# One list for attention and MLP, eight PSUM banks in one stock, key copies by transfer: windowed attention, expert attention and MLP on one core

## The chip, the core and the metric

The kernel runs on one core of a Trainium2 chip. Four engines compute, each with its own instruction queue that is worked off in order: TensorE (PE: matrix multiplications and transposes; it writes only to PSUM, which has eight banks of 128 x 512 floats), VectorE (DVE), ScalarE (ACT) and GpSimd (POOL). SyncE (SP) issues the transfers (DMA). Engines wait for each other by semaphores. The metric is the device time of one execution in microseconds (us).

## What is computed

Three stages over 4 batches of 576 tokens; every result is float32.

```python
# 1: attention, 8 heads of 64: a window of 32, in heads 4 to 7 one of 128 with every fourth key
attn = softmax(mask(q @ k.T / 8)) @ v
x = attn.transpose(0, 2, 1, 3).reshape(B, S, 512)
# 2: four experts, the two with the larger logit of x @ w_gate weighted by a softmax
for e in range(4):
    a = softmax(causal((x @ wq[e]) @ (x @ wk[e]).T / 8))
    out += weight[e] * (a @ (x @ wv[e]) @ wo[e])
# 3: norm, MLP, residual; w_ch1 (512 x 2048) and w_ch2 (2048 x 512) are float64
xn = (out - mean) / sqrt(var + 1e-6) * g_ln
y = out + relu(xn @ w_ch1) @ w_ch2
```

## The kernel before

**Number format.** A product that needs full precision is three matmuls: both factors are kept as a high and a low part (xh and xl, KH and klz, ht's two halves), and high x high, high x low and low x high are summed in one PSUM bank. Each such result so costs a copy (the high part, ACT) and a subtraction (the low part, DVE).

**Stages.** For each batch: `loads` (L301) brings q, k and v by pairs of heads; `turned_qk` (L361) transposes q and k on PE; `window` (L410) does the local attention in three units for each pair: scores (L436), maximum and subtraction (L446, L448), exponential, division, transpose (L464), the product with v (L477), and the split into xh and xl (L495, L497). `value_tile` (L505) computes V and the gate's logits in five tiles, `gate` (L551) chooses the experts, `project` (L596) makes queries and keys of a pair of experts, `attend` (L668) does one query tile of expert attention, and `out_proj` (L820) the output projection. The MLP has 18 token tiles in five groups (four of 512 tokens, one of 256) and 16 slices f of the hidden width. `decode` (L884) loads a slice of float64 weights and turns its bits into two float32 parts by a chain of steps on ACT, DVE and POOL; `norm_tile` (L992) normalizes and transposes a token tile through one buffer xg; `mlp_group` (L1025) does a pair of slices for a group: phid (L1043), ht (L1051, L1053), pout (L1068), and the sum into x2 (L1075).

**The order of the work.** Most of the kernel is a set of Python generators. Each `yield op(engine, ns, deps)` is one step with a price, `acq` takes a buffer from a pool, `key` waits for a fact, `give` and `put` return buffers and state facts. `run_chains` (L198) is a list scheduler that runs when the program is built: among all steps that could go next it emits the one with the earliest start by its own clock; ties go to the lower rank of the chain. Nothing of it runs on the chip; there each engine follows the emitted order and real waits decide. An `acq` is granted by rank as soon as the pool has a place, even where the step behind it can only start later.

**PSUM pools.** The banks are three pools: a (3) for turned q and k, window transposes and outputs, the scores of batches 1 to 3, norm tiles and the early MLP; s (2) for the window scores of batch 0 and the expert scores; t (3) for values, projections, the attend transposes and outputs, and the output projection. The value tiles of batch 0 ask for a bank right after the key V, before x and the weights exist; those of later batches wait for x first.

**Key copies.** The keys of expert ee lie in one half of the partitions of the projection's bank and must stand in both halves of KH, since the queries' high and low parts are stacked on the partitions. ACT writes one half (L643), ACT or DVE the other (L644 and L645).

**The MLP.** Units in the list: f = 0 and 1 for groups 0 to 2, then f = 2 for groups 0 to 2. All other units and the decode of f = 3 to 15 are emitted after the list by a plain loop outside the hand-written order (from L1134 on), with two s banks for phid and three t banks for pout.

Of the kernel before, what the change touches and what calls it, by code (L numbers as in the profile page):

```python
# [23 lines left out]
def windowed_attention_moe_mlp(  # L24
# [15 lines left out]
    nc = tc.nc  # L40
# [115 lines left out]
    places = {"a": [0.0] * BANKS["a"], "s": [0.0] * BANKS["s"], "t": [0.0] * BANKS["t"]}  # L156
# [17 lines left out]
    def give(tag, at, n=1):  # L174
        places[tag] += [at] * n

# [21 lines left out]
    def run_chains():  # L198
        while chains:
            again = True  # L200
            while again:
                again = False
                for c in sorted(chains, key=lambda c: c[0]):
                    kind = c[2][0]
                    if kind == "acq" and len(places[c[2][1]]) >= c[2][2]:
                        tag, n = c[2][1:]
                        places[tag].sort()
                        at = places[tag][n - 1]
                        del places[tag][:n]
                        resume(c, at)  # L210
                        again = True
                        break
# [43 lines left out]
    def attention_weights(x):  # L256
# [20 lines left out]
        t += 4000.0  # L277
# [23 lines left out]
    def loads(b):  # L301
# [4 lines left out]
        for hp in range(NHP):  # L306
# [7 lines left out]
            for x, src in enumerate((q, k)):  # L314
# [20 lines left out]
            if not dil:  # L335
                for h in range(2):
                    vs = v[b, h0 + h]
                    yield op("SP", 500.0, [t])
                    nc.sync.dma_start(vt[W:96, 0, h], vs[0:64])
                    ti = yield op("SP", 900.0, [t])  # L340
# [12 lines left out]
            land[0] = max(ti + 700.0, land[0]) + 1000.0  # L353
# [7 lines left out]
    def turned_qk(b, hp):  # L361
# [12 lines left out]
        for x in range(4):  # L374
            nat, hf = nats[x // 2], x % 2
            ta = yield acq("a")
            pt = bank("a", "ptr")
# [22 lines left out]
            give("a", t)  # L400
# [9 lines left out]
    def window(b, hp, u):  # L410
# [8 lines left out]
        tag = "s" if b == 0 else "a"  # L419
        ta = yield acq(tag)  # L420
        ps = bank(tag, "s1")
# [27 lines left out]
        give(tag, t)  # L449
# [10 lines left out]
        ta = yield acq("a")  # L460
        pt = bank("a", "ppt")
# [8 lines left out]
        give("a", t)  # L470
        ta = yield acq("a")
        po = bank("a", "po")
# [20 lines left out]
        for c0, m, sl in pieces:  # L493
            th = yield op("ACT", act(m), [t, tx])
            nc.scalar.copy(xh[:, hp, sl], po[:, c0:c0 + m])  # L495
            tl = yield op("DVE", dve(m), [th])
            nc.vector.tensor_tensor(xl[:, hp, sl], po[:, c0:c0 + m], xh[:, hp, sl].bitcast(F32), op=ALU.subtract)  # L497
        give("a", tl)
# [6 lines left out]
    def value_tile(b, i):  # L505
# [5 lines left out]
        tb = yield acq("t")  # L511
        pv = bank("t", "pv")
# [29 lines left out]
        give("t", t)  # L542
# [8 lines left out]
    def gate(b):  # L551
# [25 lines left out]
        for s in steps:  # L577
            t = yield op("DVE", 100.0, [t])
            s()
# [16 lines left out]
    def project(b, pr_):  # L596
# [18 lines left out]
        for hf in range(2):  # L615
            for wh, wl, isq in ((wkh, wkl, False), (wqh, wql, True)):
                tb = yield acq("t")
                pp = bank("t", "pp")
# [11 lines left out]
                ends = []  # L630
                for ee in range(2):
# [9 lines left out]
                    else:  # L641
                        a = yield op("ACT", 392.0, [t, tq])
                        nc.scalar.copy(KH[ee][own, cs], pp[own, :HS])  # L643
                        a2, e = yield either(("ACT", 392.0), ("DVE", 380.0), deps=[t, tq])  # L644
                        copy_by(e, KH[ee][oth, cs], pp[own, :HS])  # L645
# [3 lines left out]
                        a = max(a, a2)  # L649
                    ends.append(a)  # L650
                give("t", max(ends))
                put("q", b, pr_, hf, isq, at=max(ends))
# [15 lines left out]
    def attend(b, pr_, i):  # L668
# [19 lines left out]
        for ee in range(2):  # L688
            cuts = [(0, n)] if n <= 512 else [(0, 64), (64, n)]
            tb = yield acq("s", len(cuts))  # L690
            pss, tss = [], []
            for a, z in cuts:
                ps = bank("s", "s2")
# [6 lines left out]
                pss.append(ps)  # L700
# [14 lines left out]
            else:  # L715
# [11 lines left out]
                give("s", t, len(cuts))  # L727
                t = yield op("DVE", 75.0, [t])
                nc.vector.tensor_reduce(sm[:m, ee:ee + 1], s2[:m], axis=AX.X, op=ALU.add)
            if len(cuts) == 1:  # L730
                give("s", t)
# [16 lines left out]
        tb = yield acq("t")  # L748
        ph = bank("t", "ph")[:, :P]
# [5 lines left out]
        give("t", th)  # L755
# [3 lines left out]
        for ee in range(2):  # L759
            if i == 0:  # L760
                continue
            tb = yield acq("t")
            pt = bank("t", "ppt2")
# [9 lines left out]
            give("t", t)  # L773
# [4 lines left out]
        ty = yield key("yh", b)  # L778
        tb = yield acq("t")
        py = bank("t", "py")  # L780
# [26 lines left out]
        give("t", t)  # L807
# [12 lines left out]
    def out_proj(b, i):  # L820
# [13 lines left out]
        tb = yield acq("t")  # L834
        po = bank("t", "pwo")
# [12 lines left out]
        give("t", t)  # L848
# [16 lines left out]
    places.update(ht=[], ws=[], dsq=[], dt1=[], dpw=[], xg=[])  # L865

    def open_mlp():
# [10 lines left out]
        for tag, n in (("ht", 1), ("ws", 2), ("dsq", 1), ("dt1", 1), ("dpw", 1), ("xg", 1)):  # L878
            give(tag, t, n)
        put("wts", at=t)  # L880
# [3 lines left out]
    def decode(f, x):  # L884
# [20 lines left out]
        else:  # L905
            if f // GF % 2 == 0:
# [8 lines left out]
        ts = yield op("ACT", 610.0, [t, ta])  # L915
# [25 lines left out]
        t = yield op("ACT", 610.0, [t, tw])  # L941
# [50 lines left out]
    def norm_tile(gi, x):  # L992
# [6 lines left out]
        t, e = yield either(("ACT", 610.0), ("DVE*", 400.0), deps=[t, ta])  # L999
# [4 lines left out]
        tb = yield acq("a")  # L1004
        pt = bank("a", "pxt")
# [16 lines left out]
        give("a", max(ends))  # L1022
        put("xn", gi, x, at=max(ends))

    def mlp_group(fs, gi, htag, otag):  # L1025
# [7 lines left out]
        hs = []  # L1033
        for f in fs:
            t0 = max(t, (yield key("wf", f, 0)))
            w1h, w1l = WF[f, 0]
            tb = yield acq(htag)
            ph = bank(htag, "phid")
# [7 lines left out]
            ta = yield acq("ht")  # L1046
            pool, tag = HT.pop(0)
            ht = pool.tile([P, 2, 4 * P], F32R, tag=tag, name="ht")
            hh, hl = ht[:, 0], ht[:, 1]
# [5 lines left out]
            give(htag, th)  # L1055
            hs.append((hh, hl, th, pool, tag))
        for x, i in enumerate(grp):
            tr = yield key("rstd", i)
            tb = yield acq(otag)
            po = bank(otag, "pout")  # L1060
# [9 lines left out]
            if x == len(grp) - 1:  # L1070
                for *_, pool, tag in hs:
                    HT.append((pool, tag))
                give("ht", tp, len(hs))
            tx = yield op("DVE", 660.0, [tp, tr])
            nc.vector.scalar_tensor_tensor(x2(i), po, rstd[:, i:i + 1], x2(i), op0=ALU.mult, op1=ALU.add)  # L1075
            give(otag, tx)
            if fs[-1] == NF - 1:
                for bb, s0, p0, m in rows_of(order[i]):
# [107 lines left out]
```

## Time and profile before

| what | value |
|---|---|
| median of 3 runs (lowest, highest) | 777.85 us (777.27, 781.38) |
| the profiled execution, own time | 777.57 us |
| its span | 775.8 us |
| mean granted TensorE clock | 0.976 |
| PE busy | 728.6 us, 94% |
| DVE busy | 535.2 us, 69% |
| ACT, POOL busy | 303.4 us (39%), 207.0 us (27%) |
| bytes moved | 41.80 MB, 53 GB/s over the span |

The times in the prediction's rows are us from the start of the span; a mean or median duration in a row of groups is in ns. Busy time is the time in which an engine executes; a wait is idle time of an engine together with what ended it. The granted clock is a share of 2.4 GHz; 0.50 is the lower of its two levels, 1.2 GHz. PEld is the loading of weights into PE, SPq the queue of SP. A name such as `klz L647` is the tile that the instruction of that line writes. Line 242 is the helper `copy_by`.

### The profile page before, as it was taken

The numbers are of one execution on the slowest core, as the hardware profiler recorded it, in microseconds if no ns is written. First come the engines' busy times: TensorE is split into PE (matmuls) and PEld (weight loads), VectorE is DVE, ScalarE is ACT, GpSimd is POOL, SyncE is SP. The second block draws the span as 40 slices with busy tenths as digits, with TensorE's granted clock in tenths as the row PEclk, the third lists the DMA queues.
The fourth block names the chain that finished last, engine by engine and source line by source line (L and its number), as shares of the span: only waits on it lengthen the run. The fifth ranks groups of instructions, "written<-read, shape, count | busy, mean of one in ns | idle before, by whom it ended". The sixth has DMA issues, their size and how long they took to land.

```text
span 775.8 us, 13793 instructions
## 1 busy us (share of the span) xinstructions
PE 728.6 (94%) x5196; PEld 606.8 (78%) x5196; DVE 535.2 (69%) x1357; ACT 303.4 (39%) x817; POOL 207.0 (27%) x245
## 2 busy tenths in 40 slices
PE   6788899998999998998997999999999999999997
PEld 5677778986888686876775888888888888888886
DVE  5647898599867989898657788657466475644333
ACT  4454576466555776574325222212121121211110
POOL 3242154022302234434004445214032140220000
PEclk9869999999999999899998999999999999999999
DMA  8681143033302111011001212102011010000114
GB/s 146 123 159 31 28 102 71 21 67 74 63 17 52 39 61 55 28 52 31 1 1 55 82 54 82 55 27 82 1 55 54 26 57 27 28 1 0 41 69 136
DMA packets 87890, 41.80 MB, mean 54 GB/s; under 512 B 74384, under 2 KB 83088, under 8 KB 87824
## 3 DMA queue, kind: packets, MB, share of 16 engines
q1 hardware_dynamic: 87824, 40.92, 20.9%
q8 instruction: 41, 0.67, 0.4%
q14 instruction: 25, 0.20, 0.1%
HBM read 36.19 MB, written 4.72 MB: 53 GB/s over the span
## 4 chain that ended last, share of the span: by engine, by line
PE 71%; DVE 20%; ACT 5%; DMA 2%; issue 2%; POOL 1%; DVEq 0%; SPq 0%; ACTq 0%; POOLq 0%
PE pout L1068 26%; PE phid L1043 25%; PE pp L624 3%; PE pv L521 2%; PE pwo L840 2%; PE ppt L767 2%; PE s L436 2%; DVE nm L711 1%; PE ptr L380 1%; PE ppt L464 1%; DMA nat<-in_k_dram 1%; DVE xl L497 1%; DVE klz L647 1%; DVE sc L448 1%; DVE mx L446 1%
## 5 line engine op out<-in xcount | busy, mean ns | idle before, releaser
L1043 PE MATMUL phid<-xn,wp 128*128 128x512 f32 (+1 forms) x960 | 218.0, 374 | 2.3 <-ACT xn L1017 1.2
L1068 PE MATMUL pout<-wp,ht 128*128 128x512 f32 x864 | 216.0, 395 | 0.3 <-DVE ht L1053 0.3
L1043 PEld LDWEIGHTS phid<-xn,wp 128*128 128x128 f32 x960 | 169.7, 190 | 37.0 <-ACT xn L1017 1.6
L1068 PEld LDWEIGHTS pout<-wp,ht 128*128 128x128 f32 x864 | 159.8, 188 | 36.3 <-DVE ht L1053 0.7
L1075 DVE SCALAR_TENSOR_TENSOR x2a<-pout,rstd,x2a 128x512 f32<-128x512 f32 x124 | 88.7, 746 | 90.4 <-PE pout L1068 90.3
L1051 ACT ACTIVATE ht<-phid 128x512 fp32r<-128x512 f32 (+1 forms) x80 | 44.4, 555 | 216.5 <-PE pout L1068 138.7
L944 POOL TENSOR_TENSOR wp<-d_pw,wp 128x512 fp32r<-128x512 f32 x34 | 46.1, 1357 | 149.2 <-ACT wp L942 138.3
L1053 DVE SCALAR_TENSOR_TENSOR ht<-phid,ht 128x512 fp32r<-128x512 f32 (+1 forms) x80 | 50.1, 632 | 34.2 <-ACT ht L1051 34.2
L932 POOL TENSOR_TENSOR d_pw<-d_pw,d_t 128x512 f32<-128x512 f32 x34 | 43.9, 1290 | 78.6 <-DVE d_pw L929 70.2
L745 POOL TENSOR_SCALAR Pp<-Pp,rs 128x512 f32<-128x512 f32 (+3 forms) x38 | 45.6, 1207 | 71.0 <-DVE rs L738 37.6
L457 POOL TENSOR_TENSOR sc<-sc,rs 128x288 f32<-128x288 f32 x38 | 25.2, 668 | 86.1 <-DVE rs L455 71.7
L242 ACT COPY pT<-ppt 96x384 f32<-96x384 f32 (+4 forms) x77 | 35.2, 466 | 11.0 <-PE ppt L767 8.8
L380 PE MATMUL ptr<-ident,nat 72*128 72x72 f32 (+1 forms) x196 | 26.4, 260 | 12.9 <-DMA nat<-in_q_dram 9.6
L713 ACT ACTIVATE Pp<-s,nm 128x192 f32<-128x192 f32 (+3 forms) x64 | 30.3, 474 | 18.8 <-DVE nm L711 15.0
L942 ACT CAST wp<-d_pw 128x512 fp32r<-128x512 f32 x34 | 21.1, 620 | 40.4 <-DVE d_pw L935 33.7
L696 PE MATMUL s<-KH,SQ 128*128 128x64 f32 (+4 forms) x96 | 34.1, 362 | 1.1 <-ACT Pp L713 1.1
L436 PE MATMUL s<-kT,qT 64*64 64x96 f32 x576 | 34.4, 259 | 0.2 <-ACT kT L242 0.2
L916 ACT ACTIVATE d_sq<-ws 128x512 f32<-128x512 f32 x34 | 22.8, 672 | 28.4 <-DVE d_pw L935 22.0
L380 PEld LDWEIGHTS ptr<-ident,nat 72*128 72x128 f32 (+1 forms) x196 | 20.6, 155 | 15.4 <-DMA nat<-in_q_dram 5.2
L922 DVE SCALAR_TENSOR_TENSOR d_t<-ws,d_t 128x512 int32<-128x512 int32 x34 | 32.1, 944 | 0.6
L436 PEld LDWEIGHTS s<-kT,qT 64*64 64x64 f32 x576 | 31.7, 146 | 0.5 <-issue 0.5
L464 PE MATMUL ppt<-ident,sc 128*96 128x128 f32 x144 | 26.2, 297 | 6.0 <-DVE xl L497 3.5
(164 smaller groups left out, 1374.7 us busy)
## 6 DMA issues: line engine op xcount, KB each, us to landing
ws<-in_moe_w_ch_dram SPq DMA_DIRECT2D x34, 512.0 KB, 3.4
nat<-in_q_dram SPq DMA_DIRECT2D x14, 288.0 KB, 3.7
nat<-in_k_dram SPq DMA_DIRECT2D x14, 288.0 KB
vt<-in_v_dram SPq DMA_DIRECT2D x16, 192.0 KB, 3.7
out_dram<-x2a SPq DMA_DIRECT2D x12, 256.0 KB, 2.1
vt<-in_v_dram SPq DMA_DIRECT2D x32, 48.0 KB, 1.9
out_dram<-x2b SPq DMA_DIRECT2D x4, 256.0 KB, 2.5
vt<-in_v_dram SPq DMA_DIRECT2D x16, 40.0 KB, 2.1
```

The costliest lines, as they stand in the source:

```text
L242: (nc.scalar.copy if engine == "ACT" else nc.vector.tensor_copy)(dst, src)
L380: nc.tensor.transpose(pt[:, pw * c:pw * (c + 1)], nat[:, hf * ch + c].rearrange("p h d -> p (h d)"), ident[:pw, :pw])
L436: nc.tensor.matmul(ps[z, 96 * tt:96 * (tt + 1)], qT[z, 64 * t_:64 * t_ + 64], kT[z, 64 * t_:64 * t_ + 96], start=False, stop=tt == TU - 1)
L696: nc.tensor.matmul(ps[:m, :z - a], SQ[ee][:, q0:q0 + m], KH[ee][:, a:z], start=True, stop=False)
L745: (nc.vector if e == "DVE" else nc.gpsimd).tensor_scalar(Ps[ee][:m, 64:n], Ps[ee][:m, 64:n], rs[:m, ee:ee + 1], None, op0=ALU.mult)
L932: nc.gpsimd.tensor_tensor(pf, pf, t1.bitcast(F32), op=ALU.add)
L944: nc.gpsimd.tensor_tensor(lo, pf, hi.bitcast(F32), op=ALU.subtract)
L1043: nc.tensor.matmul(ph[:, :n_tok], ws[:, c * P:(c + 1) * P], xs[c], start=n == 0, stop=n == 3 * KC - 1)
L1051: nc.scalar.activation(hh[:, :n_tok], ph[:, :n_tok], AF.Relu)
L1053: nc.vector.scalar_tensor_tensor(hl[:, :n_tok], ph[:, :n_tok], 0.0, hh[:, :n_tok].bitcast(F32), op0=ALU.max, op1=ALU.subtract)
L1068: nc.tensor.matmul(po, a_[:, sl], w_, start=n == 0, stop=n == 3 * len(fs) - 1)
L1075: nc.vector.scalar_tensor_tensor(x2(i), po, rstd[:, i:i + 1], x2(i), op0=ALU.mult, op1=ALU.add)
```

## The change

1. `bank(name)` takes one of eight banks by number; the list's pool "bank" holds all eight, and `give_bank` returns one. Every `acq("a")`, `acq("s")` and `acq("t")` becomes `acq("bank")`.
2. The second copy of the keys is a transfer from one half of KH to the other, issued by SP, with 0.48 us for the issue and 2.2 us until it is there.
3. `attend` waits for the key yh before it takes the banks of its transposes instead of before that of its output.
4. Every unit of the MLP is a chain in the list, in a fixed order (unit n takes its ht buffer after unit n-1), and so is every decode. The weight buffers of f get pools ("w", f, x), which are returned when their last unit has used them. An ht buffer is taken before phid instead of after it.
5. Prices: loads land later in the list's clock, the first issue of a set costs 1.25 us, strided outputs of a window cost more, gate steps 0.16 instead of 0.10, ACT on 512 columns 0.665, xg on ACT 0.735 instead of 0.61.

```diff
-    BANKS = {"a": 3, "s": 2, "t": 3}
-    def bank(tag, name):
-        return ps1.tile([P, 512], F32, tag=tag, name=name, bufs=BANKS[tag])
+    NB = 8
+    taken, lent_banks = [], {}
+    def bank(name):
+        x = taken.pop(0)
+        b = ps1.tile([P, 512], F32, tag=f"bank{x}", name=name)
+        lent_banks[id(b)] = x, b
+        return b
...
+    places = {"bank": [(0.0, x) for x in range(NB)]}
+    def give_bank(b, at):
+        places["bank"].append((at, lent_banks.pop(id(b))[0]))
...
     # loads
-                ti = yield op("SP", 700.0, [t])
+                ti = yield op("SP", 780.0, [t])
-                land[0] = max(ti + 700.0, land[0]) + 1500.0
-                times.append(land[0] + 400.0)
+                land[0] = max(ti + 700.0, land[0]) + 1450.0
+                times.append(land[0] + 700.0)
-                            ti = yield op("SP", 460.0, [t])
+                            ti = yield op("SP", 460.0 if t_ else 1250.0, [t])
-            land[0] = max(ti + 700.0, land[0]) + 1000.0
+            land[0] = max(ti + 700.0, land[0] + 2100.0)
...
     # window
-            th = yield op("ACT", act(m), [t, tx])
+            wide = m if dil else 0.0
+            th = yield op("ACT", act(m) + wide, [t, tx])
...
     # value_tile
-        tb = yield acq("t")
-        pv = bank("t", "pv")
+        tb = yield acq("bank")
+        pv = bank("pv")
...
     # gate
-            t = yield op("DVE", 100.0, [t])
+            t = yield op("DVE", 160.0, [t])
...
     # project
-                        a2, e = yield either(("ACT", 392.0), ("DVE", 380.0), deps=[t, tq])
-                        copy_by(e, KH[ee][oth, cs], pp[own, :HS])
+                        a2 = yield op("SP", 480.0, [a])
+                        nc.sync.dma_start(KH[ee][oth, cs].bitcast(I32), KH[ee][own, cs].bitcast(I32))
+                        a2 += 2200.0
...
-                put("q", b, pr_, hf, isq, at=max(ends))
+                put("q", b, pr_, hf, isq, at=max(ends + dups))
...
     # attend
+        ty = yield key("yh", b)
         ta = yield acq("pTh")
...
     # out_proj
+        if last("wo", NTT):
+            for f in (2, 3):
+                for x in range(2):
+                    give(("w", f, x), tp)
...
     # decode
         else:
+            tw = yield acq(("w", f % (2 * GF), x))
...
     # norm_tile
-        t, e = yield either(("ACT", 610.0), ("DVE*", 400.0), deps=[t, ta])
+        t, e = yield either(("ACT", 735.0), ("DVE*", 400.0), deps=[t, ta])
...
-    def mlp_group(fs, gi, htag, otag):
+    def spent(f, x, t):
+        if last(("w", f, x), len(groups)) and f != GF:
+            give(("w", f % (2 * GF), x), t)
+    def mlp_group(n, fs, gi):
...
+        if n:
+            yield key("hts", n - 1)
+        unit = n
         for f in fs:
...
+            ta = yield acq("ht")
+            if f == fs[-1]:
+                put("hts", unit, at=0.0)
+            tb = yield acq("bank")
+            ph = bank("phid")
...
             if fs[-1] == NF - 1:
+                yield op("SP", 100.0, [tx])
...
-        for gi in range(EARLY):
-            chain(44.0 + gi, mlp_group((0, 1), gi, "a", "a"))
-            chain(48.0 + gi, mlp_group((2,), gi, "a", "a"))
+        jobs = [((0, 1), gi) for gi in range(EARLY)] + [((2,), gi) for gi in range(EARLY)]
+        jobs += [((0, 1), gi) for gi in range(EARLY, len(groups))]
+        jobs += [((3,), gi) for gi in range(EARLY)] + [((2, 3), gi) for gi in range(EARLY, len(groups))]
+        for f0 in range(2 * GF, NF, GF):
+            jobs += [((f0, f0 + 1), gi) for gi in range(len(groups))]
+        for n, (fs, gi) in enumerate(jobs):
+            chain(44.0 + n, mlp_group(n, fs, gi))
+        for f in range(NF):
+            need = min(n for n, (fs, gi) in enumerate(jobs) if f in fs)
+            for x in range(2):
+                chain(41.0 + f + 0.5 * x if f < 3 else 44.0 + need - 3.0 + 0.5 * x, decode(f, x))
         run_chains()
```

The loop that emitted the rest of the MLP (`run`, `weights`, `fill`) is removed.

## Rows read from the trace of the kernel before

**Rows 1.** The page: busy time, share of the span and instructions of each engine.

```profile
PE 728.6 (94%) x5196; PEld 606.8 (78%) x5196; DVE 535.2 (69%) x1357; ACT 303.4 (39%) x817; POOL 207.0 (27%) x245
```

**Rows 2.** Windows, by stage: length, busy PE, PEld, DVE, ACT, POOL, clock, DMA, GB/s.

```profile
0.00:60.00 60.00, 46.63 (x519) 39.24 (x520) 34.14 (x111) 27.74 (x74) 22.49 (x63) 0.83 0.74 138
60.00:120.00 60.00, 52.95 (x593) 45.21 (x593) 51.00 (x177) 36.44 (x117) 19.31 (x30) 0.97 0.26 53
120.00:300.00 180.00, 169.21 (x1825) 147.84 (x1823) 147.33 (x501) 111.46 (x351) 45.62 (x62) 1.00 0.23 53
300.00:408.00 108.00, 102.53 (x633) 81.50 (x630) 83.64 (x218) 50.98 (x137) 29.93 (x23) 0.97 0.08 25
408.00:430.00 22.00, 16.21 (x70) 12.11 (x70) 17.86 (x36) 10.96 (x24) 10.77 (x9) 0.84 0.22 72
430.00:771.00 341.00, 341.00 (x1569) 280.89 (x1567) 199.99 (x319) 65.86 (x117) 78.92 (x61) 1.00 0.15 47
771.00:775.80 4.80, 0.07 (x1) 0.00 (x0) 1.28 (x2) 0.00 (x0) 0.00 (x0) 1.00 0.31 119
```

**Rows 3.** Windows again, the stretches with a low granted clock; columns as in rows 2.

```profile
28.70:36.00 7.30, 7.21 (x71) 6.19 (x73) 4.08 (x11) 3.07 (x8) 0.00 (x0) 0.54 0.51 114
40.00:54.00 14.00, 13.00 (x121) 10.79 (x122) 7.06 (x21) 7.58 (x24) 5.36 (x9) 0.56 1.01 193
...
308.00:316.00 8.00, 6.93 (x30) 6.28 (x31) 6.69 (x18) 3.22 (x11) 4.39 (x4) 0.57 0.00 0
...
414.00:421.00 7.00, 5.11 (x18) 3.66 (x18) 6.04 (x12) 2.88 (x7) 3.44 (x3) 0.52 0.23 79
```

**Rows 4.** PE's waits, 60 to 400: who waited for whom, us in total, times, longest.

```profile
PE ppt L464 <- DVE xl L497: 2.7, 4, 1.3
PE pp L624 <- DVE klz L647: 2.3, 2, 1.3
PE ph L751 <- DVE Ph L740: 2.0, 3, 0.8
...
PE pxt L1008 <- DVE xn L1019: 1.7, 2, 1.2
...
PE ph L751 <- DVE yls L806: 0.2, 1, 0.2
```

**Rows 5.** Groups by line: the second key copies; busy us, mean ns, idle before.

```profile
L242 DVE CAST KH<-pp 64x288 fp32r<-64x288 f32 x18 | 8.2, 454 | 8.7 <-ACT KH L643 8.4
...
L242 ACT CAST KH<-pp 64x288 fp32r<-64x288 f32 x14 | 5.5, 394 | 0.2
```

**Rows 6.** Timeline at the last batch's gate: start, us, instruction, idle before and releaser.

```profile
302.78 1.28 DVE L571 TENSOR_TENSOR eq<-eq,tri 128x80 f32<-128x80 f32 x1
...
305.14 0.22 ACT L581 ACTIVATE ex<-ex 128x20 f32<-128x20 f32 x1 [2.07 <-DVE ex L576]
...
307.15 0.50 PE L840 MATMUL pwo<-woh,yh 128*128 128x512 f32 x1 [1.25 <-ACT yh L804]
```

**Rows 7.** Transfers by kind: count, KB each, median us from issue to landing.

```profile
ws<-in_moe_w_ch_dram SPq DMA_DIRECT2D x34, 512.0 KB, 3.4
...
vt<-in_v_dram SPq DMA_DIRECT2D x16, 192.0 KB, 3.7
...
vt<-in_v_dram SPq DMA_DIRECT2D x16, 8.0 KB, 1.7
```

**Rows 8.** Waits in SP's queue, 270 to 430: us in total, times, longest.

```profile
SPq L899 <- DVE d_pw L929: 95.8, 5, 60.0
```

**Rows 9.** Timeline of SP's queue: one set of strided value loads.

```profile
12.58 9.37 SPq L352 DMA_DIRECT2D vt<-in_v_dram  x13
```

**Rows 10.** The chain that ended last, 0 to 62: start, us, what.

```profile
52.80 5.63 PE pv L521 x45
```

**Rows 11.** Timeline of PE at the change to the MLP, columns as in rows 6.

```profile
411.21 0.65 PE L1008 MATMUL pxt<-ident,xg 128*128 128x128 f32 x4 [1.65 <-ACT xg L1001]
...
417.57 1.22 PE L1043 MATMUL phid<-xn,wp 128*128 128x512 f32 x2 [1.24 <-ACT xn L1017]
```

More of the change, by code (lines that the diff above doesn't have):

```diff
@@ L208, in run_chains @@
                         at = places[tag][n - 1]
+                        if tag == "bank":
+                            taken.extend(x for _, x in places[tag][:n])
+                            at = at[0]
                         del places[tag][:n]
@@ L276, in attention_weights @@
                 nc.sync.dma_start(st[:, :, E * D:], w_gate.rearrange("(c p) e -> p c e", p=P))
-        t += 4000.0
+        land[0] = max(t + 700.0, land[0] + (1300.0 if x == 3 else 2600.0))
+        t = land[0] + 1000.0
         n = hi.shape[2]
@@ L418, in window @@
         ts = yield acq("sc")
-        tag = "s" if b == 0 else "a"
-        ta = yield acq(tag)
-        ps = bank(tag, "s1")
+        ta = yield acq("bank")
+        ps = bank("s1")
         if dil:
@@ L629, in project @@
                     put("wqk", at=t)
-                ends = []
+                ends, dups = [], []
                 for ee in range(2):
@@ L689, in attend @@
             cuts = [(0, n)] if n <= 512 else [(0, 64), (64, n)]
[L690 to L693, printed above, removed]
+            tb = yield acq("bank", len(cuts))
+            pss, tss = [bank("s2") for _ in cuts], []
+            for (a, z), ps in zip(cuts, pss):
                 end = z == n
@@ L777, in attend @@
             give("P", t)
-        ty = yield key("yh", b)
-        tb = yield acq("t")
-        py = bank("t", "py")
+        tb = yield acq("bank")
+        py = bank("py")
         t = yield op("PE", 218.0 * (i + 1), tts + [tb], "columns")
@@ L833, in out_proj @@
             yield key("fr", b, (ti - NTA) // 2)
-        tb = yield acq("t")
-        po = bank("t", "pwo")
+        tb = yield acq("bank")
+        po = bank("pwo")
         n = 0
@@ L865, in windowed_attention_moe_mlp @@
     places.update(ht=[], ws=[], dsq=[], dt1=[], dpw=[], xg=[])
+    places.update({("w", f, x): [] for f in range(4) for x in range(2)})
     def open_mlp():
@@ L879, in open_mlp @@
             give(tag, t, n)
+        for f in range(GF):
+            for x in range(2):
+                give(("w", f, x), t)
         put("wts", at=t)
@@ L1036, in mlp_group @@
             w1h, w1l = WF[f, 0]
-            tb = yield acq(htag)
-            ph = bank(htag, "phid")
+            ta = yield acq("ht")
+            pool, tag = HT.pop(0)
+            ht = pool.tile([P, 2, 4 * P], F32R, tag=tag, name="ht")
+            hh, hl = ht[:, 0], ht[:, 1]
+            if f == fs[-1]:
+                put("hts", unit, at=0.0)
+            tb = yield acq("bank")
+            ph = bank("phid")
             n = 0
@@ L1045, in mlp_group @@
                     n += 1
[L1046 to L1049, printed above, removed]
+            spent(f, 0, tp)
             th = yield op("ACT", act(n_tok), [tp, ta])
@@ L1106, in windowed_attention_moe_mlp @@
         chain(40.0, open_mlp())
-        for f in range(3):
-            for x in range(2):
-                chain(41.0 + 2 * f + x, decode(f, x))
         chain(41.5, inverse_std(0, 4 * EARLY))
@@ L1115, in windowed_attention_moe_mlp @@
                 chain(41.2 + gi + 0.1 * x, norm_tile(gi, x))
-        for gi in range(EARLY):
-            chain(44.0 + gi, mlp_group((0, 1), gi, "a", "a"))
-            chain(48.0 + gi, mlp_group((2,), gi, "a", "a"))
-        run_chains()
-    def run(gen):
-        ask = next(gen)
-        while True:
-            value = 0.0
-            if ask[0] == "op" and len(ask[1]) > 1:
-                value = 0.0, ask[1][0][0]
-            try:
-                ask = gen.send(value)
-            except StopIteration:
-                return
-    jobs = [((0, 1), gi) for gi in range(EARLY, len(groups))]
-    jobs += [((3,), gi) for gi in range(EARLY)] + [((2, 3), gi) for gi in range(EARLY, len(groups))]
-    for f0 in range(2 * GF, NF, GF):
-        jobs += [((f0, f0 + 1), gi) for gi in range(len(groups))]
-    def weights(fs):
-        for f in fs:
-            for x in range(2):
-                run(decode(f, x))
-                yield
-    fill = weights((3,))
-    for x, (fs, gi) in enumerate(jobs):
-        if (fs[-1], 0) not in WF:
-            for _ in fill:
-                pass
-        if x == 0 or fs != jobs[x - 1][0]:
-            if fs != (2, 3):
-                for _ in fill:
-                    pass
-                nf = fs[-1] + 1 if fs[-1] > 1 else 3
-                fill = weights(range(nf, min(nf + GF, NF)) if nf > 3 else (3,))
-        next(fill, None)
-        run(mlp_group(fs, gi, "s", "t"))
+        jobs = [((0, 1), gi) for gi in range(EARLY)] + [((2,), gi) for gi in range(EARLY)]
[7 more added lines that the diff above has]
+            need = min(n for n, (fs, gi) in enumerate(jobs) if f in fs)
+            for x in range(2):
+                chain(41.0 + f + 0.5 * x if f < 3 else 44.0 + need - 3.0 + 0.5 * x, decode(f, x))
+        run_chains()
 _INS = ['q', 'k', 'v', 'moe_w_gate', 'moe_wq', 'moe_wk', 'moe_wv', 'moe_wo', 'moe2_g_ln', 'moe2_w_ch1', 'moe2_w_ch2']
```

79 lines of the change are left out of this document (40 added, 39 removed).

## The prediction

> **What bounds the kernel now.** I read the page first: TensorE (PE) is busy 728.6 of 775.8 us, so it is idle for 47.2 us, and no other engine comes near it over the whole span [rows 1]. That share hides where the 47 us lie, so the next view is the busy time by stage [rows 2]. The stages are: the first batch's windows while loads arrive (0 to 60), the batches' attention (60 to 408), the change to the MLP (408 to 430), the MLP (430 to 771), the last transfers (771 to the end). PE's idle time by stage is the stage's length less its busy time: 13.4, 7.1, 10.8, 5.5, 5.8, 0.0 and 4.7 us. Two things are to be seen. From 430 to 771 there is nothing to win: PE is busy 341.00 of 341 us. And in attention DVE (51.00 of 60, 147.33 of 180) is nearly as full as PE, so what frees DVE may count there.
>
> The second loss does not look like idle time. TensorE's granted clock is 0.5 to 0.6 in four stretches [rows 3], partly or wholly at its lower level, 1.2 instead of 2.4 GHz, each time after PE had stood still for a few us. The busy time in such a stretch times one less the clock is what it cost: 7.21 x 0.46 = 3.3 us, 13.00 x 0.44 = 5.7 us, 6.93 x 0.43 = 3.0 us and 5.11 x 0.48 = 2.5 us, 14.5 us in all. An idle gap that is closed so pays twice.
>
> Third, what ended PE's waits between 60 and 400 us [rows 4]. In twelve of these rows (first 2.7, last 0.2 us) the releaser is the last reader of a PSUM bank: xl, klz, xn, ht, SQ, V, yl or yls. Together they are 12.1 us, half of that stretch's 23 us. A PE wait on "DVE klz" by a projection is no data: the bank still holds the last projection. This is a shortage inside pools of three and two banks.
>
> **The change, part by part.**
>
> *One stock of eight banks.* Up to 12.1 us of waits are at stake [rows 4]. They will not all go: a wait that ends earlier is followed by the next, usually the data of the same step (Ph, pT, sc stand in the same view with 2.0 us and less). I take two thirds, -8.0 us; bounds -12.1 and 0.
>
> *The same stock in the first batch.* The five value tiles of batch 0 ask for their bank before anything else does, as their key V is there from the start, while their weights are not: all 45 first matmuls of L521 run at 52.80 [rows 10]. Before, they could take only the three banks of pool t, and the windows had five of their own; now they hold five, and the windows, score tiles and turned keys of 0 to 52 us share three. By the list's own prices a window holds a bank for 0.64 + 0.36 + 0.38 us (scores, maximum, subtraction), 0.34 + 0.48 (transpose, copy) and 0.34 + 0.33 + 0.28 (output, two copies), 3.2 us and with hand-overs about 4, and a turn about 1; a head pair (three windows, four turns) so needs some 16 us of bank, 5.3 us with three banks always full; a pair's loads take 5 to 10 us, the strided values alone 9.37 us to issue [rows 9]. So loads still set the pace, but with little to spare. I take +1 us; bounds -2 (loads now booked later, so an order nearer to what arrives) and +5.
>
> *Second key copies as transfers.* There are 32: 18 on DVE (8.2 us) and 14 on ACT (5.5 us) [rows 5]. 13.7 us of engine time go, but PE's remaining waits on these engines are short; I take -1, bounds 0 and -3. Against it stands the path of the copy: 0.45 us on DVE become an issue on SP and a landing. No row shows a transfer inside SBUF; of loads, 8 KB land in 1.7 us and 192 KB in 3.7 us [rows 7]. 64 x 288 x 4 bytes are 74 KB, between them but nearer to the small one, so some 2.2 us, which is what the list books. The first score of each of the eight (batch, pair) groups waits for it; PE has other chains then. I take +2 us for all; bounds 0 and +6. The Trainium skill, "DMA: Bandwidth & Descriptors", Anatomy of one DMA, gives a fixed cost of about 2.0 us, most of it the receipt of the write, and a rate of 436 GB/s, fitted on another issuing path; as an estimate from that page a copy would be 2.2 us and the sum the same; no row here shows such a transfer.
>
> *Prices of gate and loads.* The gap at 306 to 310 starts in the gate: a step booked at 0.1 us takes 1.28, ACT stands 2.07 us in its queue for the exponential, and PE then waits 1.25 us for yh behind it [rows 6]. With the 2.2 us of idle and the 3.0 us at the low clock that gap is worth 5.2 us. The gate's steps are now booked at 0.16; I take half, -2.6, bounds 0 and -5.2.
>
> *The MLP in the list, and the gap at 408.* There PE waits for normalized tiles that share one buffer xg: 1.65 us before one tile, 1.24 us before the first phid [rows 11]. Idle and clock together are 5.8 + 2.5 = 8.3 us. The list doesn't cut this chain: the work of the first three token groups that can run early (units 0 to 5) is unchanged and is used up, and unit 6 needs just these tiles. The decode of f = 3 now starts only when the last output projection is placed, so its DVE steps fall into the same gap. ACT's xg is booked dearer, so DVE takes more of them. I take -0.5; bounds +2 and -5. From 430 on the list can only equal a PE that is always busy; DVE has 199.99 busy of 341 us [rows 2], so a late ht should be rare: +0.5, bounds 0 and +4. The last transfers stay.
>
> *Sum:* -8.0 + 1 - 1 + 2 - 2.6 - 0.5 + 0.5 = -8.6 us. The profiled execution took 777.57 us (span 775.8), so 769.0; the median of the runs is 0.28 above it, so **769.3 us**.
>
> **The rivals.**
>
> *Gaps only move (about 776.5).* A new plan has its own mismatches between booked and real times; each new hole of 2 to 3 us brings 2.5 to 3.3 us at the low clock with it [rows 3]. Two of them at 5.5 us eat the gain, and so would the upper bound of the first batch with half the bank term. For it: decode's and vector steps are still booked short, and 13 issues booked at 6.8 us take 9.37 [rows 9]. Against it: bank waits are a shortage, which more banks remove in any order.
>
> *The load queue holds up the keys (slower, about 785).* SP issues in order and stands on a wait: the MLP's weight loads stood 95.8 us in five waits for their buffer, the longest 60 us [rows 8]. A key copy placed behind such a load, or behind a strided value load, is as late as that load's buffer is later than planned; PE has the scores next in its order, stands, and loses the clock. Price: some 2.5 us idle and 3 us at the low clock, 5.5 us for each of the eight groups hit. From the sum without the +2 (767.3) it takes 781.7 - 767.3 = 14.4 us, three groups, to be slower than before by half a per cent: 783.8 us. Against it: the list places copies by time, so only misjudged times hurt. The Trainium skill says on the same page and section that transfers don't wait on semaphores themselves, the issuing sequencer does; [rows 8] agree.
>
> *The gap at 408 closes too (about 760).* If the list brings the four tiles' norm steps forward of the decode steps, the 8.3 us go, with two thirds of the gate's gap: 769.3 - 8 - 1 = 760. For it: DVE does decode steps between the norm steps there now. Against: one buffer xg, unchanged.
>
> **How the numbers follow.** Forecast 0.47, larger gain 0.11, gaps only move 0.24, load queue 0.18. About half a per cent (3.9 us) is what a measurement of this kernel can tell from no change. Faster is the first two, 0.58; same 0.24; slower 0.18. The low end is 758, a little below the larger gain; the bounds of the terms reach lower, but not all together. The high end, 783, takes in the moved gaps and the load queue with fewer than three groups hit. About 2 in 10 are left out, most of it above.
>
> **What would show it.** Right: PE waits on bank readers between 60 and 400 below 4 us; no KH copies on DVE or ACT; DVE busy 8 us less; no gap at the last batch's gate; MLP from its start still without PE idle. Wrong: PE waits named by a transfer into KH; SP waits of several us ahead of key copies; PE idle over 16 us before 60; a gap longer than 16 us, or new low-clock stretches, at the start of the MLP; PE waits on ht after it. What makes the forecast wrong most easily is a hole in the new plan where none was before, as its price is double.

## The result and the profile after

The changed kernel takes 769.75 us (median of 4 runs, 769.32 to 770.02), the kernel before 777.89; the ratio is 0.9886, with a 95% interval of 0.9856 to 0.9915. The profiled execution took 770.02 us, its span is 768.2 us. The forecast was 769.3.

First the page's line of busy times, to be held against [rows 1], then the busy time by stage, against [rows 2] (length, busy PE, PEld, DVE, ACT, POOL, clock, DMA share, GB/s):

```profile
PE 726.0 (94%) x5196; PEld 603.8 (79%) x5196; DVE 529.5 (69%) x1342; ACT 297.0 (39%) x793; POOL 192.0 (25%) x233
```

```profile
0.00:60.00 60.00, 46.87 (x523) 39.63 (x524) 37.16 (x119) 28.24 (x73) 20.66 (x63) 0.86 0.77 143
60.00:120.00 60.00, 55.95 (x616) 47.20 (x615) 50.63 (x189) 38.78 (x127) 15.13 (x22) 1.00 0.28 59
120.00:300.00 180.00, 170.28 (x1839) 148.70 (x1837) 146.93 (x493) 103.10 (x320) 39.79 (x58) 0.99 0.27 61
300.00:380.00 80.00, 73.54 (x452) 58.45 (x452) 63.43 (x175) 44.66 (x123) 31.50 (x25) 0.98 0.10 31
380.00:432.00 52.00, 47.12 (x264) 37.25 (x260) 34.84 (x65) 19.00 (x40) 12.72 (x10) 0.97 0.11 33
432.00:768.20 336.20, 332.19 (x1517) 272.61 (x1515) 196.53 (x305) 63.26 (x112) 72.24 (x57) 1.00 0.15 47
```

PE's idle time is now 42.2 us instead of 47.2. The second loss, busy time at the lower clock, is had from windows of 2 us as the sum of busy time times one less the clock: 12.7 instead of 16.0 us. What is left of the span without both, 713.2 and 712.6 us, is busy time counted at full clock. So the gain is 5.0 us less idle and 3.3 us less at the low clock. In the kernels below this rest is 710 to 717 us for the same 5,196 matmuls, and nothing here shows why; so a difference of a few us between two kernels can't be read from the two losses alone. By stage, idle plus clock loss, before and after:

| stage, us | before | after |
|---|---|---|
| 0 to 60 | 13.4 + 8.9 | 13.1 + 8.1 |
| 60 to 120 | 7.0 + 1.7 | 4.0 + 0.0 |
| 120 to 300 | 10.8 + 0.0 | 9.7 + 1.7 |
| 300 to 380 | 5.5 + 3.0 | 6.5 + 1.5 |
| 380 to 432 | 5.8 + 2.5 | 4.9 + 1.4 |
| 432 to the end | 4.7 + 0.0 | 4.0 + 0.0 |

More than half comes from 60 to 120. Of the 4.7 us there, 1.7 are a stretch at the low clock in the kernel before, from 90 us on, after 2 us in which PE was busy for 0.74 us. The prediction's four stretches [rows 3] leave it out (columns as above):

```profile
90.00:92.00 2.00, 2.00 (x12) 1.78 (x13) 1.24 (x5) 0.90 (x5) 0.00 (x0) 0.50 0.13 29
```

The last matmul of the last output projection starts at 401.6 instead of 408.7 us; from there to the end it is 366.6 us after and 367.1 before. All of the gain but 0.5 us is made before the end of attention.

These are stages of one execution each, and the stages of two executions can differ with the order of the work unchanged. The changed kernel and the one with the late MLP outside the list (below) have the same order on every engine up to 343 us; their losses are 21.2 and 15.8 us from 0 to 60, 4.0 and 4.4 from 60 to 120, 11.4 and 14.2 from 120 to 300.

PE's waits from 60 to 400 us (who waited for whom, us in total, times, longest), against [rows 4]:

```profile
PE ph L765 <- DVE rs L748: 2.9, 1, 2.9
PE ppt L475 <- POOL sc L468: 2.5, 5, 1.0
...
PE pp L636 <- DVE klz L660: 0.7, 2, 0.6
...
PE pp L636 <- DVE SQ L650: 0.5, 2, 0.3
```

The waits on bank readers, xl and klz at the head of the view before, are nearly gone: the releasers of the prediction's list that are no data of the waiting matmul come to 1.9 us instead of 12.1. Others head the view now: ph waits for its own data, and ppt for sc. For all kernels I count a wait as a bank wait where the tile that ended it is one that a DVE or ACT step writes while it empties a bank, and is not read by the waiting matmul, and every other one as another wait, mostly for data. This rule takes in more than the prediction's list (the exponential Pp, the copies kT, qT, pT, pTh, G, the sum x2a), and it goes by the names that the view gives, which are inferred. It gives 13.6 of 22.3 us before and 5.8 of 19.8 us after. The bank waits fell by 7.8, all waits by 2.5 us.

### The profile page after: what moved, and what is told of

Same layout as the page of the kernel before. It is cut to its first block, busy times and chain, and to the rows that moved or that the text cites. A ratio compares the mean times of both kernels' runs of the same rounds, so it can differ in the third digit from the quotient of the medians.

```text
span 768.2 us, 13813 instructions
## 1 busy us (share of the span) xinstructions
PE 726.0 (94%) x5196; PEld 603.8 (79%) x5196; DVE 529.5 (69%) x1342; ACT 297.0 (39%) x793; POOL 192.0 (25%) x233
## 4 chain that ended last, share of the span: by engine, by line
PE 70%; DVE 20%; ACT 4%; issue 2%; SPq 2%; DMA 1%; POOL 1%; DVEq 0%; POOLq 0%; ACTq 0%
PE pout L1102 25%; PE phid L1080 25%; PE pp L636 3%; PE pv L533 3%; PE pwo L853 2%; DVE nm L722 2%; DVE sm L464 2%; DVE mx L457 1%; DVE sc L459 1%; DVE SQ L650 1%; PE po L488 1%; PE ptr L392 1%; PE s L447 1%; PE ppt L475 1%; PE ppt L781 1%
## 5 line engine op out<-in xcount | busy, mean ns | idle before, releaser
L1102 PE MATMUL pout<-wp,ht 128*128 128x512 f32 x864 | 219.7, 395 | 1.5 <-DVE ht L1087 1.3
L1111 DVE SCALAR_TENSOR_TENSOR x2a<-pout,rstd,x2a 128x512 f32<-128x512 f32 x124 | 92.2, 748 | 60.9 <-PE pout L1102 59.9
L955 POOL TENSOR_TENSOR d_pw<-d_pw,d_t 128x512 f32<-128x512 f32 x32 | 41.3, 1291 | 180.1 <-DVE d_pw L952 145.0
L468 POOL TENSOR_TENSOR sc<-sc,rs 128x288 f32<-128x288 f32 x35 | 23.3, 672 | 136.0 <-DVE rs L466 117.3
L967 POOL TENSOR_TENSOR wp<-d_pw,wp 128x512 fp32r<-128x512 f32 x32 | 44.4, 1389 | 36.4 <-ACT wp L965 36.4
L757 POOL TENSOR_SCALAR Pp<-Pp,rs 128x512 f32<-128x512 f32 (+3 forms) x34 | 39.3, 1163 | 52.6 <-DVE rs L750 39.8
L965 ACT CAST wp<-d_pw 128x512 fp32r<-128x512 f32 x32 | 19.8, 619 | 47.2 <-DVE d_pw L958 41.3
L253 ACT COPY pT<-ppt 96x384 f32<-96x384 f32 (+4 forms) x74 | 33.5, 462 | 11.1 <-PE ppt L781 6.3
L781 PE MATMUL ppt<-ident,Pp 128*128 128x128 f32 x160 | 28.8, 282 | 2.8 <-DVE rs L748 1.1
L709 PE MATMUL s<-klz,SQ 128*128 128x64 f32 (+4 forms) x96 | 30.8, 321 | 0.0
```

Source lines behind the costliest of these rows:

```text
L757: (nc.vector if e == "DVE" else nc.gpsimd).tensor_scalar(Ps[ee][:m, 64:n], Ps[ee][:m, 64:n], rs[:m, ee:ee + 1], None, op0=ALU.mult)
L781: nc.tensor.transpose(pt[:, P * (j - 1):P * j], Ps[ee][:, k0:k0 + P], ident)
L955: nc.gpsimd.tensor_tensor(pf, pf, t1.bitcast(F32), op=ALU.add)
L967: nc.gpsimd.tensor_tensor(lo, pf, hi.bitcast(F32), op=ALU.subtract)
L1102: nc.tensor.matmul(po, a_[:, sl], w_, start=n == 0, stop=n == 3 * len(fs) - 1)
```

## The experiments

Two theories stood against each other. One: the parts carry the gain, by the terms of the prediction's sum, the shared banks above all. The other: the list gives another order with every edit, and orders differ by some us whatever the edit is. The kernels that undo one part come first, then those that do one part alone, then edits that mean nothing. No kernel undoes part 3 of the change (`attend` waits for yh before its banks) or the new order rules of the early MLP units.

**The three pools again, all else changed.**

```diff
-    NB = 8
-    places = {"bank": [(0.0, x) for x in range(NB)]}
+    BANKS = {"a": 3, "s": 2, "t": 3}
+    places = {tag: [(0.0, x) for x in range(n)] for tag, n in BANKS.items()}
...
-        tb = yield acq("bank")
+        tb = yield acq("t")          # and "a", "s" where they stood before
```

> The changed kernel with its eight banks cut into the three pools of before again (a 3, s 2, t 3; early MLP on a, the rest on s and t); all else as changed. Theory 1 (the shared banks carry the gain, sum -8 + 1 us): about 776.7 us, and 8 us of PE waits on bank readers (xl, klz, SQ, xn, yl) back between 60 and 400 us. Theory 2 (the gain is from ACT and DVE relieved of the key copies, or from prices): within 2 us of 769.8. Theory 3 (no part carries it; every new order of the list falls a few us here or there): anything from 766 to 778 without more bank waits.

773.5 us (ratio to before 0.9939, 0.9918 to 0.9961): half of what the sum booked. The bank waits are all back, 12.8 of 23.1 us.

**The key copies on ACT or DVE again.**

```diff
-                        a2 = yield op("SP", 480.0, [a])
-                        nc.sync.dma_start(KH[ee][oth, cs].bitcast(I32), KH[ee][own, cs].bitcast(I32))
-                        a2 += 2200.0
+                        a2, e = yield either(("ACT", 392.0), ("DVE", 380.0), deps=[t, tq])
+                        copy_by(e, KH[ee][oth, cs], pp[own, :HS])
```

> The changed kernel with the second key copy on ACT or DVE again. Theory 1 (sum -1 for the engines, +2 for the landing): about 768.8 us, KH copies back on DVE and ACT with some 13 us. Theory 2 (the relief of DVE carries the gain): 774 us or more. Theory 3: 766 to 778, the new order decides.

775.8 us (0.9973, 0.9951 to 0.9995), where the sum said 768.8. Read alone, this would make the transfers the part that carries the gain; a second order of the same kernel, below, forbids that. What does stand is a link that the prediction hadn't seen: the copy on an engine also keeps the projection's bank, and bank waits are 8.1 us with eight shared banks (9.3 in the second order).

**All prices as before.**

```diff
-                ti = yield op("SP", 780.0, [t])
+                ti = yield op("SP", 700.0, [t])
...
-            t = yield op("DVE", 160.0, [t])
+            t = yield op("DVE", 100.0, [t])
...
-        t, e = yield either(("ACT", 735.0), ("DVE*", 400.0), deps=[t, ta])
+        t, e = yield either(("ACT", 610.0), ("DVE*", 400.0), deps=[t, ta])
...
```

> The changed kernel with all prices of the list as before (loads, strided outputs, gate steps, ACT on 512 columns, xg). Theory 1 (sum -2.6 for the gate's gap, nothing elsewhere but the head's order): about 772.4 us, with a gap of PE of several us near the last batch's gate again. Theory 2 (prices are what aligns the plan with the chip, and carry the gain): 775 us or more, with PE waits all over 60 to 400. Theory 3: 766 to 778.

772.1 us (0.9919, 0.989 to 0.9948). The time is the one expected, the reason isn't there: from 300 to 380 this kernel, with the gate's old price, has 2.3 us idle and no low clock, the changed one 6.5 + 1.5.

**The late MLP outside the list.**

```diff
         jobs = [((0, 1), gi) for gi in range(EARLY)] + [((2,), gi) for gi in range(EARLY)]
-        jobs += [((0, 1), gi) for gi in range(EARLY, len(groups))]
-        jobs += [((3,), gi) for gi in range(EARLY)] + [((2, 3), gi) for gi in range(EARLY, len(groups))]
-        for f0 in range(2 * GF, NF, GF):
-            jobs += [((f0, f0 + 1), gi) for gi in range(len(groups))]
...
-        for f in range(NF):
...
+        for f in range(3):
...
+        # after the list: the loop of before, the banks in turn over all eight
+        run(mlp_group(2 * EARLY + x, fs, gi))
```

> The changed kernel with only the early MLP units (f 0 to 2 on groups 0 to 2) and the decode of f 0 to 2 in the list; the rest is emitted after it by the loop of before, the banks in turn over all eight. Theory 1 (sum -0.5 + 0.5): 769.8 us within 1.5, attention until the last output projection as in the changed kernel, and the gap at the start of the MLP the same within 2 us. Theory 2 (the list closes part of that gap): 772 us or more, all of the difference between 400 and 430 us.

771.1 us (0.9922, 0.9894 to 0.995), within the 1.5 us. The order of PE is that of the changed kernel for its first 3,565 matmuls, to 402 us; the last matmul of the last output projection starts at 400.6 us, and from 430 to 760 PE is busy 330.00 of 330 us. The list gives the MLP nothing that the loop did not.

**The transfers alone, on the kernel before.** The edit is the second one, the other way round.

> The kernel before with one part alone: the second key copies as transfers. By the prediction's sum (-1 for the engines, +2 for the landing): 778.6 us, no gain. If the relief of DVE and ACT carries most of the gain, as the 775.8 us of the changed kernel with engine copies suggests: about 772 us, with less PE idle where DVE is fullest. If its gain exists only with the shared banks: 777 to 778.

781.0 us (1.0033, 1.0016 to 1.005): no gain.

**The shared banks alone, on the kernel before.** The edit is the first one, the other way round. Part 3 and the order rules of the early MLP units stay in as changed, so it is the banks with these two.

> The kernel before with the eight shared banks alone: no transfers of keys, old prices, the late MLP outside the list. The prediction's terms for it (-8 + 1): 770.9 us, and 8 us less of PE waits on bank readers between 60 and 400 us. If the banks pay only where the key copies are off the engines: 776 us or more, the bank waits gone all the same and others in their place.

783.1 us (1.0066, 1.0045 to 1.0087), against 770.9 by the sum: the prediction's main term gains nothing without the other parts; this order is slower. PE's waits from 60 to 400 us in this kernel:

```profile
PE ppt L474 <- POOL sc L467: 5.2, 6, 1.6
PE py L800 <- DVE pT L253: 2.3, 3, 1.2
...
PE ph L763 <- DVE Ph L750: 1.5, 2, 0.9
...
PE ppt L474 <- DVE xl L508: 0.8, 2, 0.4
PE ppt L474 <- DVE klz L658: 0.8, 1, 0.8
```

The bank waits are down to 4.9 us, from 13.6, and all waits are 25.4, from 22.3. PE stands no less than before; it now waits mostly for sc, pT and Ph, the results of the steps themselves.

**Edits that mean nothing.** The list's price for a switch of PE's tiling is 141 ns. Another value by 1 to 3 ns says nothing about the chip, but it changes ties: in the kernels below, between 1,071 and 2,648 of PE's 5,196 matmuls stand elsewhere in its order.

```diff
-    MODE = 141.0
+    MODE = 140.0     # or 138, 139, 142
```

The changed kernel with 140 and with 138:

> The changed kernel with the same meaningless change (140 instead of 141 ns), which gives another order on all engines. If the gain is the parts' and not the luck of one order: 768 to 772 us. If orders differ by chance by as much as the gain: outside of that.

> The changed kernel with 138 ns, a third order of it after 769.75 and 763.9 us. If the gain is the parts': 762 to 772 us. If orders differ by as much as the gain: above 774 us.

763.9 us (ratio to before 0.9813, 0.9786 to 0.984) and 776.7 us (0.9979, 0.9958 to 1.0001). The kernel before with 139 and with 142:

> The kernel before with a change that means nothing (139 instead of 141 ns for a switch of PE's tiling in the list), which gives another order of PE. If the gain of 8 us is the parts': 774 to 782 us, as the two orders known without shared banks in all (777.9, 781.0). If before was only an unlucky order: 771 us or less.

> As n_before_139 with 142 ns, a third order of the kernel before. The gain is the parts': 774 to 782 us. Before was an unlucky order: 771 us or less.

780.9 us (1.0039, 1.002 to 1.0058) and 785.7 us (1.0093, 1.0063 to 1.0124). The kernel with engine copies, with 142:

> u_dup (engine copies) with a change that means nothing: the list's price for a switch of PE's tiling is 142 instead of 141 ns, which gives another order of some 2700 of PE's lines. If the 6 us lost in u_dup come from the copies on the engines: 774 to 777.5 us. If they are the luck of one order: anything, 769 us included.

771.5 us (0.9912, 0.9889 to 0.9934), after 775.8 with 141.

So three orders of the kernel before take 777.9, 780.9 and 785.7 us, three of the changed one 769.75, 763.9 and 776.7. The medians do not overlap, and the means, 781.5 and 770.1, are 11 us apart; but the spread inside each is 8 and 13 us, as large as the gain. The slowest of the changed ones can't be told from the kernel before (776.7 to 777.9, a ratio of 0.9958 to 1.0001), and single executions overlap: 770.0 to 778.1 us with 138 ns, 773.6 to 781.8 for the kernel before, over 29 of them. Three against three would fall this way round by chance once in 20 times. Of the four new orders three fell outside the range expected if the parts alone decide: 763.9, 776.7 and 785.7. All four experiments that undo a part lie between 771 and 776 us, inside the spread of the changed kernel's own orders, and tell nothing of that part's share. The two that do a part alone lie inside the spread of before.

**Later banks for the first value tiles.**

```diff
-        if b > 0:
-            for c in range(KC):
-                yield key("x", b, c)
+        for c in range(KC):
+            yield key("x", b, c)
         tb = yield acq("bank")
```

> The changed kernel, in which the value tiles of batch 0 ask for their banks after x is there, as those of the other batches do. The prediction booked +1 us (bounds -2 and +5) for five banks held from the start. If that is right: about 768.8 us, and less PE idle before 52 us. If the head waits for loads only: 769.8 within 1.5, with the same PE idle before 52 us.

780.5 us (1.0033, 1.0012 to 1.0054), 11 us more than the changed kernel. Its first 60 us, in the columns of the stages:

```profile
0.00:60.00 60.00, 46.57 (x488) 40.03 (x488) 33.84 (x108) 24.45 (x64) 18.08 (x58) 0.77 0.71 135
```

PE is busy as long as in the changed kernel, but at a clock of 0.77 instead of 0.86. The first projection starts at 71.1 instead of 59.7 us, though after 617 matmuls instead of 521; PE's 500th matmul starts at 62.8 instead of 57.3. So this order does not show the banks held from the start as a cost. Whether they help by keeping later windows from going ahead of the value tiles, or whether this order or this execution is an unlucky one, stays open.

All kernels in one table. The losses and waits are those of the profiled execution, whose own time stands beside the median and can lie 5 us from it. Losses are sums over windows of 2 us; the last columns are PE's waits from 60 to 400 us by the rule above.

| kernel | median us | profiled us | PE idle | clock loss | bank waits | all waits |
|---|---|---|---|---|---|---|
| before | 777.9 | 777.6 | 47.2 | 16.0 | 13.6 | 22.3 |
| before, 139 ns | 780.9 | 781.9 | 48.6 | 17.6 | 13.0 | 25.0 |
| before, 142 ns | 785.7 | 785.7 | 51.6 | 15.6 | 7.5 | 26.8 |
| transfers alone | 781.0 | 777.7 | 48.9 | 10.4 | 9.7 | 24.6 |
| banks alone | 783.1 | 784.3 | 53.4 | 13.0 | 4.9 | 25.4 |
| changed | 769.75 | 770.0 | 42.2 | 12.7 | 5.8 | 19.8 |
| changed, 140 ns | 763.9 | 759.0 | 38.0 | 7.6 | 2.2 | 21.0 |
| changed, 138 ns | 776.7 | 776.2 | 46.7 | 17.4 | 2.7 | 21.0 |
| three pools | 773.5 | 772.8 | 46.6 | 10.4 | 12.8 | 23.1 |
| engine copies | 775.8 | 778.5 | 47.4 | 18.3 | 8.1 | 25.1 |
| engine copies, 142 ns | 771.5 | 768.1 | 44.0 | 9.0 | 9.3 | 26.0 |
| old prices | 772.1 | 771.2 | 45.7 | 13.3 | 5.0 | 17.5 |
| late MLP outside | 771.1 | 770.9 | 43.4 | 12.7 | 5.8 | 19.6 |
| later value banks | 780.5 | 783.8 | 49.0 | 21.4 | 4.4 | 22.5 |

The profiled time follows idle and clock loss together, to within the 7 us by which the rest of the span differs. It does not follow the bank waits: 7.5 us of them go with 785.7 us, 12.8 with 773.5. The fastest of all is the changed kernel with 140 ns, 763.9 us, 14 us below before; that is one of three orders, and what in it is the change and what the order is not shown.

## Why the prediction was right, and where its steps were not

**The number** came within half a us, and the change is faster in the sense that its three orders as a set are below the three of before. That the number fits so well is luck: two other orders of the same source lie 6 us below and 7 us above it.

**Shared banks, -8.0 us: the step that failed.** What it says of the waits was right to the size: by the wider rule 7.8 us of bank waits went (13.6 to 5.8), by the prediction's own list 10.2 (12.1 to 1.9, below the 4 us named as a sign). That PE would have this time was wrong: all its waits from 60 to 400 us fell by 2.5 us. Where bank waits went others came, 13.6 and 8.7 us before, 5.8 and 14.0 after; alone the banks gained nothing (783.1 us). The reservation in the text, that a wait that ends earlier is followed by the next, was the main thing and not the correction. One stage is an exception, from 60 to 120; it comes last below.

**The first batch, +1 us: not settled.** Without the early hold the kernel was slower in the one order that was tried. In the changed kernel the stage is 1.1 us better than before (13.4 + 8.9 to 13.1 + 8.1), inside the bounds. Two kernels point the other way, the one that was feared: PE's 500th matmul starts at 62.1 us with the banks alone and at 57.8 before, at 54.0 with three pools and at 57.3 in the changed kernel. But the late MLP outside, with the same order as the changed kernel, has it at 52.6, so that differences of 4 to 5 us here can be the execution's.

**Key copies, -1 and +2 us: not settled.** Undone, they cost 6.0 us in one order and 1.7 in the other. DVE is busy 5.7 us less, not 8. The side that was feared did not come. In the changed kernel no wait of PE names a transfer into KH, and the copies' own rows, first the instruction in SP's queue (ns min, median, max), then SP's longest waits in it, show why:

```profile
L657 SPq DMA_DIRECT2D KH<-KH x32: 461/494/1350, 62.0 to 312.0; - x32
```

```profile
SPq L921 <- DVE d_pw L952: 183.9, 14, 30.6
...
SPq L657 <- ACT KH L655: 49.1, 17, 13.6
```

SP does stand for long on weight loads, as [rows 8] did, but most key copies wait only for their own source, KH from ACT: 30 of the 32 are issued within 0.3 us of its end. The two others stood behind value loads for 1.7 and 3.0 us, the latter here, its source ready at 162.25:

```profile
157.32 7.87 SPq L364 DMA_DIRECT2D vt<-in_v_dram  x13
165.29 1.14 SPq L657 DMA_DIRECT2D KH<-KH  x2
```

The issue is 0.49 us, booked at 0.48. By the updates of the copies' semaphores in the trace a copy has landed 2.0 us after its issue began (median; longest 3.4); the list books 2.7 for issue and landing together. So the prediction's 2.2 us, which it could only place between the rows of other transfers, was near.

**Gate and prices, -2.6 us: the gap was there again.** From 300 to 380 idle and clock loss are 8.0 us after 8.5. PE's wait behind the gate [rows 6] is gone, though the gate has a long step again, now booked at 0.16 us, and some us later PE stands for another chain's data. The timeline (start, us, instruction, idle before and releaser) has the gate's step, three steps of that chain and the wait:

```profile
300.40 1.32 DVE L584 TENSOR_TENSOR gt<-gt,eq 128x80 f32<-128x80 f32 x1
...
310.36 0.16 DVE L748 RECIPROCAL rs<-sm 128x2 f32<-128x2 f32 x1
...
313.24 0.38 DVE L750 TENSOR_TENSOR rs<-rs,gw 128x2 f32<-128x2 f32 x1
...
314.22 0.28 DVE L752 TENSOR_TENSOR Ph<-Pp,rs 128x128 f32<-128x128 f32 x1
...
314.64 0.30 PE L765 MATMUL ph<-ident,Ph 128*128 128x128 f32 x1 [2.89 <-DVE rs L748]
```

What PE needs is Ph, which ends at 314.50; the releaser that the view names is a later rs, the step that ends next. The steps of Ph's chain stand in DVE's queue among those of decode, projection and scores, 2.7 us between two of them. That is the rival "gaps only move" at work, the low clock behind it included. (Its 776.5 us did not follow from its terms: two holes at 5.5 us on the forecast make 780.3.)

**The gap at 408, -0.5 us, and the MLP, +0.5 us: sizes about right, one reason wrong.** The stage 380 to 432 went from 8.3 to 6.3 us, and from 432 on PE is idle for the last transfers and less than 0.2 us besides. But the prediction held that the gap must stay, since the early units are used up. The kernel with engine copies and 142 ns shows that this is the list's choice; its stages 300 to 380 and 380 to 432:

```profile
300.00:380.00 80.00, 70.28 (x463) 55.06 (x462) 64.20 (x182) 47.70 (x130) 29.12 (x23) 0.96 0.10 34
380.00:432.00 52.00, 51.96 (x264) 42.30 (x263) 37.67 (x69) 19.52 (x39) 14.19 (x11) 1.00 0.13 41
```

and PE at the change to the MLP:

```profile
397.16 0.60 PE L1030 MATMUL pxt<-ident,xg 128*128 128x128 f32 x4
397.51 0.94 PE L1101 MATMUL pout<-wp,ht 128*128 128x512 f32 x3
398.30 0.85 PE L1079 MATMUL phid<-xn,wp 128*128 128x512 f32 x3
398.99 0.87 PE L1101 MATMUL pout<-wp,ht 128*128 128x512 f32 x3
399.72 0.66 PE L1030 MATMUL pxt<-ident,xg 128*128 128x128 f32 x4
```

Here early units are left and fill the time between the norm tiles; PE is busy 51.96 of 52 us at full clock. They were missing earlier instead, where 9.7 us are idle. The work that can fill is fixed, and it closes one gap or the other.

**Where the gain is seen** is the stage 60 to 120 (8.7 to 4.0 us), in which the three orders of the changed kernel have 4.0 to 4.8 us idle and those of before 6.3 to 7.0. That stage, the first projections and attends, is the one place, but for some tenths at the very end, where idle time is less in every order. PE's waits in it, first two of the kernel before, then two of the changed one:

```profile
PE pp L624 <- DVE klz L647: 2.3, 2, 1.3
PE ppt L464 <- DVE xl L497: 1.8, 2, 1.3
```

```profile
PE s L708 <- issue: 1.4, 2, 0.8
PE ppt L781 <- DVE rs L750: 0.9, 1, 0.9
```

Here the bank waits did go without as much in their place: 5.0 of 6.8 us before (4.3 and 3.3 in its other orders), 1.3 of 3.8 us after (1.6 and 1.6), and the other waits are 1.8 to 3.4 us before and 2.5 to 2.8 after. With shared banks and the old prices the bank waits of this stage go as well (1.6 us with the banks alone, 1.4 with old prices), but other waits are 7.5 and 5.1 us, and idle 8.8 and 7.1. That would fit banks that pay only where the list's prices of loads are near the real ones; but later value banks, with all prices as changed, has 6.1 us of other waits and 7.2 idle, and three pools and engine copies have 5.4 to 5.7 idle. Which part does it is not shown.

## What to carry to other kernels

A wait that the profile puts down to a buffer is worth its length only if the data behind it is ready; look at what the same instruction would have waited for next. Where a list or a scheduler gives the order, time an edit that means nothing as well, in two or three variants on both sides: here it was worth 6 us down and 7 us up, and no single part of a change of 8 us could be told apart from it. Work that can fill gaps is a stock; say where it would go if it doesn't go here.

## What the runs showed of the hardware that was not expected

After a transfer that landed 2 us later, PE was 4.6 us behind. The changed kernel and the one with the late MLP outside have the same order on every engine up to 343 us. Their turned queries of the second batch (timeline of PE) and the window from 40 to 54 us (columns as above), first the changed kernel:

```profile
41.10 0.44 PE L392 MATMUL ptr<-ident,nat 96*128 96x96 f32 x3 [3.20 <-DMA nat<-in_q_dram]
```

```profile
40.00:54.00 14.00, 12.00 (x112) 10.44 (x113) 7.37 (x21) 6.91 (x20) 4.71 (x9) 0.63 0.99 186
```

then the one with the late MLP outside:

```profile
39.14 0.44 PE L392 MATMUL ptr<-ident,nat 96*128 96x96 f32 x3 [1.11 <-DMA nat<-in_q_dram]
```

```profile
40.00:54.00 14.00, 12.19 (x151) 11.13 (x151) 10.33 (x34) 9.48 (x29) 9.12 (x16) 1.00 0.97 193
```

The load of these queries was issued at 35.22 and 34.85 us and landed, by its semaphore's updates in the trace, at 40.97 and 39.00. After a wait of 3.20 us the granted clock of the window is 0.63, after one of 1.11 it stays at 1.00, and in the same busy time PE has done 151 matmuls instead of 112. The first value tile runs at 52.4 and 47.8 us. At the last output projection 1.0 us of these 4.6 us is left (401.6 and 400.6): what follows has waits and low-clock stretches of its own that use the lead up. It is one execution of each.
